# Retention, routing and two expert layers: placing split into two steps, state products and scores in 64x64 tiles

## The chip, the cores and the metric

The kernel runs on one core of a Trainium2 chip. The metric is the device time of one launch in microseconds (us), the median of several runs of the same kernel. Beside it stands one profiled execution, from which all durations below are taken.

## What is computed

```python
def _attn_ref(q, k, v):                      # 8 batches, 8 heads, 576 positions, 64 wide
    scores = scale * np.matmul(q, k.transpose(0, 1, 3, 2))
    Dmat = np.where(rel >= 0, gamma[:, None, None] ** rel[None, :, :], 0.0)
    return np.matmul(scores * Dmat[None, :, :, :], v)

def _moe_ref(x, w_gate, w1, w2):             # 4608 tokens, 512 wide, 8 experts, 1024 hidden
    logits = x @ w_gate
    expert_idx = np.argmax(logits, axis=1)
    ...
        ye = np.maximum(xe @ w1[e], 0.0) @ w2[e]
        out[mask] = gate_w[mask, None] * ye

def _moe2_ref(x, w_in, w_out):               # 512 -> 2048 -> 512
    h = x @ w_in
    return (h * np.cos(h)) @ w_out
```

The three run one after the other: retention, a layer in which each token goes to the one expert with the largest logit, and a wide layer with h cos(h) between its products.

## The kernel before

The retention stage walks over 40 chunks, five for each batch: four of 128 positions and one of 64 (`CH`, line 31). A loop of 45 rounds (line 495) issues the work of several chunks by hand, and each engine runs its instructions in the order in which they are issued. Round i does, in this order:

- `transposes(i + 1)`: eight transposes on TensorE (PE), copied out by ScalarE (ACT) as `qT` and `kpT`;
- `scores(i)`: eight products of keys and queries, one for each head. Two heads share the 128 partitions, so a head's operands lie in partitions 0 to 63 or 64 to 127, and the outputs go to the two banks of `sc` by that half. VectorE (DVE) then masks each bank into `pT` (line 299);
- `decay_k(i + 2)` on DVE, and in rounds 20 to 27 `unit_split`, which waits for weights of the next layer (`wst`) on ACT;
- `inter(i - 1)`: the state of the earlier chunks times the queries. The state of a pair of heads is kept block-diagonal in a 128x128 tile `sbd`, whose other half is zeros, so that four full 128x128 products do it (line 313);
- `intra(i - 1)`: `v` times `pT`, added into the same bank `xps`; DVE scales it into `xt` (line 325); then, but for a batch's last chunk, the state's update in `S` (line 329), which ACT copies into the two diagonal blocks of `sbd` in two copies;
- `table`, then `place`, where a batch is due;
- `rows(i - 2)`: TensorE turns `xt` back into rows and takes the logits (line 340), in the same two banks as `scores` (tag `sc`, one buffer). ACT copies the rows out as `xs`, then DVE reduces the logits to `lgt` (line 344), then SyncE's queue (SP) stores the rows to `xd`;
- `route(i - 2)` at the end of a batch: five short DVE steps that find each token's expert;
- the loads of q, k, v of chunk i + 4, and in rounds 18 to 25 one of weights, on SP's queue.

`scores(i + 1)` of the next round writes the banks that `lgt` of this round reads, and so has to wait for it.

`place` takes a batch one round after it was routed: matmuls with ones and a triangle give each token's rank in `lg` (lines 376 to 384); DVE makes the slot (lines 388 to 400); GpSimd (POOL) and DVE make the one-hot tiles `oh` and `rt` (lines 401 to 425); DVE adds to the running count (lines 429 to 437). Two rounds later `table` multiplies the one-hot tiles together into `lg` (line 444) and DVE adds the result to a table. The batches are placed in rounds 7, 12, 17, 22, 27, 32 and 37 (the last batch in three pieces, in rounds 39, 40 and 42).

After the loop the expert layers run on gathered rows, and then the wide layer. Float32 products that are not transposes appear in the trace as two matmul records each.

Of the kernel before, what the change touches and what calls it, by code (L numbers as in the profile page):

```python
# [11 lines left out]
F32 = mybir.dt.float32  # L12
# [5 lines left out]
ALU = mybir.AluOpType  # L18
AX = mybir.AxisListType
# [3 lines left out]
P = 128  # L23
H = 8
D = 64
DM = 512
E = 8
# [3 lines left out]
CH = [(0, 128), (128, 128), (256, 128), (384, 128), (512, 64)]  # L31
# [8 lines left out]
NWARM = 28  # L40
NWARM2 = 16
# [27 lines left out]
def const_table(B):  # L69

    NT = B * SEQ
    t = np.zeros((P, C_END), np.float64)
    p = np.arange(P)
    t[:, C_ID:C_ID + 128] = np.eye(128)
    t[:, C_MASK:C_MASK + 128] = p[:, None] <= p[None, :]
    t[:, C_TRI:C_TRI + 128] = p[:, None] < p[None, :]
    t[:, C_ONE:C_ONE + 128] = 1.0
    t[:, C_IOTA:C_IOTA + 128] = p
    gam = 1.0 - 2.0 ** (-5.0 - np.arange(H))

    hp = 2 * np.arange(4)[None, :] + (p >= D)[:, None]
# [22 lines left out]
def attn_moe_kernel(ctx, tc, q, k, v, wg, w1, w2, win, wout, ctab, out):  # L104
# [81 lines left out]
    def warm(n, bank, t):  # L186
        t = t.bitcast(BF16)
        for _ in range(n):
            mm(out=bank[:, :2 * P], lhsT=t[:, :P], rhs=t, start=True, stop=True)


    with ExitStack() as actx:
# [25 lines left out]
        def setup():  # L218
            nc.vector.tensor_copy(out=tri, in_=cc(C_TRI, P))
            nc.vector.tensor_copy(out=ones, in_=cc(C_ONE, P))  # L220
            nc.vector.tensor_copy(out=rbase, in_=cc(C_BASE, E))
            nc.vector.memset(rsb, 0.0)
            nc.vector.tensor_copy(out=wgi[:, :, 0:P], in_=ident.unsqueeze(1).to_broadcast([P, 4, P]))
            nc.vector.tensor_copy(out=wgi[:, :, P:RW], in_=wgs)

        def decay_table(c):
# [8 lines left out]
            xts.append(t)  # L235
        sbd = []
        for i in range(2):
            t = ap1.tile([P, 4, P], F32, name=f"sbd{i}")
            nc.gpsimd.memset(t, 0.0)
            sbd.append(t)  # L240
        lgt = []
        for i in range(2):
            t = ap1.tile([P, NCH, E], F32, name=f"lgt{i}")
# [41 lines left out]
        def scores(i):  # L285
            b, c = steps[i]
            o, n = CH[c]
            s = st[i]
            pT = ap2.tile([P, H, P], F32, tag="pT", name="pT")
            two = ps1.tile([P, 8, P], F32, tag="sc", name="sc")  # L290
            scs = [two[:, 0:4], two[:, 4:8]]
            for a in range(4):
                for g in range(2):
                    r = 64 * g
                    mm(out=scs[g][:n, a, :n], lhsT=s["kpT"][r:r + 64, a, :n], rhs=s["qT"][r:r + 64, a, :n],
                       start=(a == 0), stop=True, skip_group_check=True)
# [5 lines left out]
        sps = ps1.tile([P, 4, D], F32, tag="S", name="S")  # L302


        def inter(i):
            b, c = steps[i]
            o, n = CH[c]
            s = st[i]
            s["xp"] = ps2.tile([P, 4, P], F32, tag="x", name="xps")
            if c > 0:  # L310
                sb = sbd[(i - 1) % 2]
                for j in range(4):
                    mm(out=s["xp"][:, j, :n], lhsT=sb[:, j, :], rhs=s["qT"][:, j, :n], start=(j == 0), stop=False,
                       skip_group_check=True)

        def intra(i):
            b, c = steps[i]
            o, n = CH[c]
            s = st[i]
            xp = s["xp"]  # L320
            for h in range(H):
                r = D * (h % 2)
                mm(out=xp[r:r + D, h // 2, :n], lhsT=s["v"][:n, h, :], rhs=s["pT"][:n, h, :n],
                   start=(c == 0 and h < 2), stop=True, skip_group_check=True)
            nc.vector.tensor_mul(out=xts[i % 3][:, :, :n], in0=xp[:, :, :n], in1=gx[:, c, :, :n])
            if c < NCH - 1:
# [42 lines left out]
        def place(i0, n, ohb, df):  # L369
# [28 lines left out]
            nc.vector.tensor_scalar(out=ge, in0=dd, scalar1=0.0, scalar2=None, op0=ALU.is_ge)  # L398
            hot = ap2.tile(hs, F32, tag="hot", name="hot")
            nc.vector.scalar_tensor_tensor(out=hot, in0=dd, scalar=float(P), in1=ge, op0=ALU.is_lt, op1=ALU.mult)  # L400
# [25 lines left out]

            if not last:
                gates()
            if n > 2:
                rr = ap2.tile([P, E], F32, tag="rr", name="rr")  # L430
                nc.vector.tensor_reduce(out=rr, in_=ohb[:, :n - 1].rearrange("p c e -> p e c"), axis=AX.X, op=ALU.add)
                nc.vector.tensor_add(out=rsum, in0=rsum, in1=rr)
            elif n == 2:
                nc.vector.tensor_add(out=rsum, in0=rsum, in1=ohb[:, 0, :])
            m = CH[c0 + n - 1][1]
            nc.vector.tensor_add(out=rsum[:m], in0=rsum[:m], in1=ohb[:m, n - 1, :])
            nc.vector.tensor_copy(out=rsb, in_=rsum)

            def enter(k0, k1):
                w = (k1 - k0) * SL  # L440
# [26 lines left out]
        groups[NS - 3] = (NS - 3, 1)  # L467
        groups[NS - 1] = (NS - 2, 2)
        routed = []
        tabled = []  # L470

        load(0, "q")
# [9 lines left out]
        nc.sync.dma_start(out=wgs, in_=wg.rearrange("(c p) e -> p c e", p=P))  # L482
# [6 lines left out]
        warm(NWARM, ps2.tile([P, 512], F32, tag="x", name="xps"), idle)  # L489
# [4 lines left out]
        waiting = []  # L494
        for i in range(NS + 5):
            if i + 1 < NS:
                transposes(i + 1)
            if i < NS:
# [5 lines left out]
            if i == 0:  # L504
                setup()
            if 1 <= i <= NS:
                inter(i - 1)
                intra(i - 1)

            prev, waiting[:], tabled[:] = waiting[:], tabled[:], []  # L510
# [2 lines left out]
            if i >= NS + 2:  # L513
                while waiting:
                    table(*waiting.pop(0))
            prev, routed[:] = routed[:], []
# [11 lines left out]
        assert not tabled and not routed and not waiting  # L528
        assert not tabled and not routed
        rp = ps2.tile([P, 512], F32, tag="x", name="xps")  # L530
        mm(out=rp[:, :E], lhsT=ones, rhs=rsb, start=True, stop=True)
        warm(NWARM2, ps2.tile([P, 512], F32, tag="x", name="xps"), ident)
        nc.vector.tensor_copy(out=cnt, in_=rp[:, :E])
        nc.vector.tensor_copy(out=sidf, in_=sid)

# [499 lines left out]
```

## Time and profile before

| | us |
|---|---|
| median of 3 runs | 1568.36 (1565.32 to 1570.71) |
| the profiled execution | 1571.7, of which the span is 1569.8 |

The trace is read by stage: a table of windows gives the busy time of every engine in a stretch, the timeline gives the instructions of one round in order, and the table of waits says what an engine stood idle for. All times are us from the start of the span.

### The profile page before, as it was taken

To read this page: it belongs to the slowest core of one execution; us is meant where nothing else is said; L and a number is where in the kernel's file an instruction comes from. 1 tells how busy PE (TensorE), PEld (TensorE's weight loads), DVE (VectorE), ACT (ScalarE), POOL (GpSimd) and SP (SyncE) were. 2 spreads that over 40 slices of the span, in tenths; PEclk is the share of its full clock that TensorE was granted. 3 is DMA by queue.
4 is the path that set the end of the run, shared out by engine and by line. 5 is a ranking of instruction groups with operands and counts; after the bars stand their busy time and mean duration, and the time that the engine had idled before them with its cause. 6 is when DMAs were issued, how large, how long until landed. Compare 5 with 4: busy or idle time off the path is not lost.

```text
span 1569.8 us, 24472 instructions
## 1 busy us (share of the span) xinstructions
PE 1502.7 (96%) x9565; PEld 1334.4 (85%) x9565; DVE 896.1 (57%) x1618; ACT 781.1 (50%) x1395; POOL 359.3 (23%) x399
## 2 busy tenths in 40 slices
PE   8997798799999999999999999999999999999998
PEld 7887788699999999999878888888888888888886
DVE  3555655556575665652256656666665656666554
ACT  3334332244445445433266666666565666666654
POOL 3111111365666657562000101010000101010101
PEclk9999899699999999999999999999999999999999
DMA  9768763365657556556640100000010100000000
GB/s 184 161 146 186 182 136 88 104 203 190 201 188 226 195 182 237 180 162 213 218 162 28 48 7 34 21 27 28 1 53 1 54 1 28 0 27 1 28 0 27
DMA packets 168520, 163.10 MB, mean 104 GB/s; under 512 B 119012, under 2 KB 127664, under 8 KB 166352
## 3 DMA queue, kind: packets, MB, share of 16 engines
q1 hardware_dynamic: 155696, 110.50, 25.8%
q0 software_dynamic: 10688, 36.31, 6.6%
q10 hardware_dynamic: 2016, 14.68, 2.8%
q8 instruction: 76, 1.25, 0.3%
q14 instruction: 44, 0.36, 0.1%
HBM read 115.70 MB, written 45.76 MB: 103 GB/s over the span
## 4 chain that ended last, share of the span: by engine, by line
issue 42%; PE 4%; POOL 2%; ACT 1%; DVE 1%; DMA 0%; POOLq 0%; SPq 0%
PE hps L907 2%; POOL out_dram L959 2%; PE acc L949 1%; PE acc L951 1%; PE acc L950 1%; DVE sa L918 0%; ACT ka L915 0%; DVE sa L919 0%; ACT sa L921 0%; ACT sa L922 0%; POOL spare L140 0%; DVE ka L917 0%; DMA yin<-ydT 0%; ACT sa L923 0%; DVE gl L934 0%
## 5 line engine op out<-in xcount | busy, mean ns | idle before, releaser
L907 PE MATMUL hps<-yT,wunit 128*128 128x512 f32 x1728 | 417.5, 391 | 0.4 <-ACT yT L894 0.4
L907 PEld LDWEIGHTS hps<-yT,wunit 128*128 128x128 f32 x1728 | 324.9, 188 | 69.8 <-DVE yT L895 1.3
L949 PE MATMUL acc<-wunit,gh 128*128 128x512 f32 x576 | 224.1, 389 | 0.0
L950 PE MATMUL acc<-wunit,gh 128*128 128x512 f32 x576 | 224.1, 389 | 0.0
L951 PE MATMUL acc<-wunit,gl 128*128 128x512 f32 x576 | 224.1, 389 | 0.0
L621 PE MATMUL hps<-hh,wunit 128*128 128x360 f32 (+1 forms) x1024 | 223.6, 310 | 0.0
L606 PE MATMUL hps<-xT,wunit 128*128 128x360 f32 (+1 forms) x1536 | 222.8, 306 | 0.5 <-ACT xT L591 0.5
L606 PEld LDWEIGHTS hps<-xT,wunit 128*128 128x128 f32 x1536 | 220.6, 190 | 1.2 <-ACT xT L591 0.9
L959 POOL DMA_INDIRECT out_dram<-orow,perm x36 | 35.2, 978 | 808.7 <-DVE orow L955 802.3
L929 DVE TENSOR_TENSOR sa<-hps,sa 128x512 f32<-128x512 f32 x144 | 99.3, 690 | 160.2 <-ACT sa L923 160.2
L921 ACT ACTIVATE sa<-sa 128x512 f32<-128x512 f32 x144 | 91.1, 633 | 193.8 <-DVE sa L919 193.8
L698 POOL TENSOR_TENSOR wunit<-wst,wunit 128x512 fp32r<-128x512 f32 x112 | 157.6, 1426 | 89.6 <-ACT wunit L697 89.4
L621 PEld LDWEIGHTS hps<-hh,wunit 128*128 128x128 f32 x1024 | 172.1, 192 | 0.0
L621 PE MATMUL hps<-hl,wunit 128*128 128x360 f32 (+1 forms) x512 | 158.1, 309 | 4.8 <-DVE hl L610 4.8
L610 DVE SCALAR_TENSOR_TENSOR hl<-hps,hh 128x360 fp32r<-128x360 f32 (+1 forms) x128 | 60.6, 474 | 178.1 <-ACT hh L609 178.1
L915 ACT ACTIVATE ka<-hps,biases 128x512 f32<-128x512 f32 x144 | 99.0, 688 | 69.4 <-PE hps L907 69.4
L951 PEld LDWEIGHTS acc<-wunit,gl 128*128 128x128 f32 x576 | 108.2, 188 | 22.5
L950 PEld LDWEIGHTS acc<-wunit,gh 128*128 128x128 f32 x576 | 108.1, 188 | 22.5
L949 PEld LDWEIGHTS acc<-wunit,gh 128*128 128x128 f32 x576 | 108.2, 188 | 22.4
L623 ACT COPY yev<-hps 128x256 f32<-128x256 f32 (+1 forms) x64 | 26.7, 417 | 169.1 <-issue 93.9
L923 ACT ACTIVATE sa<-sa,biases 128x512 f32<-128x512 f32 x144 | 104.1, 723 | 4.7
L917 DVE TENSOR_SCALAR ka<-ka 128x512 f32<-128x512 f32 x144 | 61.0, 424 | 74.2 <-ACT ka L915 74.2
(148 smaller groups left out, 2055.5 us busy)
## 6 DMA issues: line engine op xcount, KB each, us to landing
wst<-in_moe_w_dram SPq DMA_DIRECT2D x64, 512.0 KB, 4.5
wd<-cvo POOLq DMA_DIRECT2D x32, 512.0 KB, 3.9
wunit<-wd ACTq DMA_DIRECT2D x14, 1024.0 KB, 5.9
yin<-ydT SPq DMA_DIRECT2D x36, 256.0 KB, 2.7
ldq<-in_q_dram SPq DMA_DIRECT2D x32, 256.0 KB, 3.5
ldk<-in_k_dram SPq DMA_DIRECT2D x32, 256.0 KB, 4.2
ldv<-in_v_dram SPq DMA_DIRECT2D x32, 256.0 KB, 4.5
xd<-xs SPq DMA_DIRECT2D x32, 256.0 KB, 2.2
```

Source lines behind the costliest of these rows:

```text
L606: mm(out=ph[:, :n], lhsT=u[:, a, kc, f0:f0 + P], rhs=t[:, bq, kc, :n], start=(idx == 0), stop=(idx == 11))
L621: mm(out=py[:, :n], lhsT=u[:, w], rhs=t[:, :n], start=(fc == 0 and g == 0), stop=(fc == 7 and g == 2))
L698: nc.gpsimd.tensor_sub(out=u[:, 1, 2 * g + c], in0=s[:, c], in1=u[:, 0, 2 * g + c])
L907: mm(out=ph, lhsT=u[:, a, kc, f0:f0 + P], rhs=t[:, bq, kc, :], start=(idx == 0), stop=(idx == 11))
L915: nc.scalar.activation(out=ka, in_=ph, func=AF.Identity, scale=INV2PI, bias=magic)
L921: nc.scalar.activation(out=sa, in_=sa, func=AF.Sin, scale=0.5)
L923: nc.scalar.activation(out=sa, in_=sa, func=AF.Identity, scale=-2.0, bias=one)
L929: nc.vector.tensor_mul(out=sa, in0=ph, in1=sa)
L949: mm(out=a, lhsT=gh[:, s], rhs=u[:, 0, fc % 4], start=(fc == 0), stop=False)
L950: mm(out=a, lhsT=gh[:, s], rhs=u[:, 1, fc % 4], start=False, stop=False)
L951: mm(out=a, lhsT=gl[:, s], rhs=u[:, 0, fc % 4], start=False, stop=(fc == 15))
L959: ins = nc.gpsimd.indirect_dma_start(out=out[:, :], out_offset=bass.IndirectOffsetOnAxis(ap=perm[:, k:k + 1], axis=0), in_=o, in_offset=None)
```

## The change

- **Placing.** `place` keeps the ranks, the slots and the running count. The rest (the reduction `rm`, the one-hot tiles, the gates) becomes `spread`, which for all but the last piece runs one round later. The steps that make `dd`, `ge` and `hot` move from DVE to POOL for these pieces, one of them cut into two. In a round, `rows` and `route` now come ahead of `spread` and `place`.
- **Scores** are issued as 64x64 tiles: four matmuls for each pair of heads, two for a chunk of 64.
- **State products** are issued head by head as 64x64 tiles. The state is kept without its zeros (`sbd` is 128x4x64, one ACT copy of all partitions). So that four neighbouring heads fall on four different tiles, odd head pairs write the other half of the partitions, and in a second bank; `xps` now has two banks and one buffer instead of two buffers of one bank.
- The halves of odd pairs stay swapped through `xt`; the decay table, the identity in `wgi` and the gate weights are swapped to suit, so one DMA of the gate weights becomes three and one copy into `wgi` three.
- Where the chunk i - 1 has 64 positions, `inter(i - 1)` moves to the front of the round, followed by a small ACT copy out of `xps` (`between`).

```diff
-            for a in range(4):
-                for g in range(2):
-                    r = 64 * g
-                    mm(out=scs[g][:n, a, :n], lhsT=s["kpT"][r:r + 64, a, :n], rhs=s["qT"][r:r + 64, a, :n],
-                       start=(a == 0), stop=True, skip_group_check=True)
+            for j in range(4):
+                for g, r in ((0, 0), (1, D), (0, D), (1, 0)):
+                    if r < n:
+                        mm(out=scs[g][r:r + D, j, :n], lhsT=s["kpT"][D * g:D * g + D, j, r:r + D],
+                           rhs=s["qT"][D * g:D * g + D, j, :n], start=(j == 0), stop=True, skip_group_check=True)
...
+        def place_of(h):
+            j, a = h // 2, h % 2
+            return (j % 2) * 4 + j // 2, D * (a ^ (j % 2))
...
-            s["xp"] = ps2.tile([P, 4, P], F32, tag="x", name="xps")
+            s["xp"] = ps1.tile([P, 8, P], F32, tag="x", name="xps")
             if c > 0:
                 sb = sbd[(i - 1) % 2]
-                for j in range(4):
-                    mm(out=s["xp"][:, j, :n], lhsT=sb[:, j, :], rhs=s["qT"][:, j, :n], start=(j == 0), stop=False,
-                       skip_group_check=True)
+                for h in range(H):
+                    k, r = place_of(h)
+                    d = D * (h % 2)
+                    mm(out=s["xp"][r:r + D, k, :n], lhsT=sb[d:d + D, h // 2, :], rhs=s["qT"][d:d + D, h // 2, :n],
+                       start=(h < 4), stop=False, skip_group_check=True)
...
             for h in range(H):
-                r = D * (h % 2)
-                mm(out=xp[r:r + D, h // 2, :n], lhsT=s["v"][:n, h, :], rhs=s["pT"][:n, h, :n],
-                   start=(c == 0 and h < 2), stop=True, skip_group_check=True)
-            nc.vector.tensor_mul(out=xts[i % 3][:, :, :n], in0=xp[:, :, :n], in1=gx[:, c, :, :n])
+                k, r = place_of(h)
+                mm(out=xp[r:r + D, k, :n], lhsT=s["v"][:n, h, :], rhs=s["pT"][:n, h, :n],
+                   start=(c == 0 and h < 4), stop=True, skip_group_check=True)
...
-                nc.scalar.copy(out=t[0:64, :, 0:64], in_=sps[0:64])
-                nc.scalar.copy(out=t[64:128, :, 64:128], in_=sps[64:128])
+                nc.scalar.copy(out=t, in_=sps)
...
-            nc.vector.tensor_tensor(out=dd, in0=dst.unsqueeze(2).to_broadcast(hs), in1=lo, op=ALU.subtract)
+            ve.tensor_tensor(out=dd, in0=dst.unsqueeze(2).to_broadcast(hs), in1=lo, op=ALU.subtract)
...
+            nc.vector.tensor_copy(out=rsb, in_=rsum)
+            if not last:
+                placed.append((i0, n, ex, hot, dd, False))
+
+        def spread(i0, n, ex, hot, dd, last):
...
+            short = 1 <= i <= NS and CH[steps[i - 1][1]][1] <= D
+            if short:
+                inter(i - 1)
+                nc.scalar.copy(out=between, in_=st[i - 1]["xp"].rearrange("p (a j) t -> p j a t", a=2)[:, 0:2, :, 0:1])
             if i + 1 < NS:
                 transposes(i + 1)
...
-            for r in prev:
-                place(*r)
             if 0 <= i - 2 < NS:
                 rows(i - 2)
+            to_spread, placed[:] = placed[:], []
+            to_place, routed[:] = routed[:], []
             if i - 2 in groups:
                 route(*groups[i - 2])
+            for r in to_spread:
+                spread(*r)
+            for r in to_place:
+                place(*r)
```

## Rows read from the trace of the kernel before

**Rows 1.** Windows by stage: length, busy time (instructions) by engine, PEclk, DMA share, GB/s.
```profile
22.00:268.26 246.26, 216.00 (x2568) 194.63 (x2567) 135.69 (x339) 85.95 (x186) 37.49 (x72) 0.92 0.68 153
268.26:298.00 29.74, 18.27 (x153) 15.07 (x153) 17.81 (x93) 5.05 (x11) 8.53 (x17) 0.69 0.32 98
298.00:770.00 472.00, 462.84 (x3241) 460.46 (x3241) 260.09 (x392) 197.07 (x415) 261.53 (x212) 0.98 0.58 191
```

**Rows 2.** Waits from 22 to 268: who for whom, total us, times, longest.
```profile
PE sc L295 <- DVE lgt L344: 29.4, 13, 3.7
ACT wunit L179 <- DMA wst<-in_moe_w_dram: 14.2, 6, 4.8
```

**Rows 3.** Timeline of PE, one ordinary round: start, length, operation, shapes, records.
```profile
27.75 1.16 PE L295 MATMUL sc<-qT,kpT 64*128 64x128 f32 x16 [0.26 <-DVE lgt L344]
28.84 1.16 PE L313 MATMUL xps<-qT,sbd 128*128 128x128 f32 x8
29.93 1.09 PE L323 MATMUL xps<-pT,ldv 128*64 128x128 f32 x16
30.86 0.64 PE L329 MATMUL S<-ldv,kp 128*64 128x64 f32 x16
31.42 1.19 PE L340 MATMUL rw<-wgi,xt 128*128 128x136 f32 x8
32.45 0.60 PE L279 MATMUL tp<-ct,ldq 128*128 128x128 f32 x4
...
33.52 0.56 PE L295 MATMUL sc<-qT,kpT 64*64 64x64 f32 x12
```

**Rows 4.** Timeline of DVE and ACT in the same round.
```profile
28.96 1.29 DVE L299 TENSOR_TENSOR pT<-sc,ca 128x512 f32<-128x512 f32 x2 [1.26 <-PE sc L295]
32.65 0.59 ACT L343 COPY xs<-rw 128x512 f32<-128x512 f32 x1 [0.30 <-PE rw L340]
33.27 0.19 DVE L344 TENSOR_REDUCE lgt<-rw 128x8 f32<-128x32 f32 x1 [1.44 <-ACT xs L343]
```

**Rows 5.** Timeline of PE and DVE around the placing of one batch.
```profile
117.03 1.17 PE L340 MATMUL rw<-wgi,xt 128*128 128x136 f32 x8
117.21 0.20 DVE L388 TENSOR_TENSOR t<-lg,ohb 128x40 f32<-128x40 f32 x1
119.46 0.36 DVE L403 TENSOR_REDUCE rm<-dd 128x5 f32<-128x200 f32 x1 [0.72 <-POOL dd L401]
120.92 0.20 DVE L431 TENSOR_REDUCE rr<-ohb 128x8 f32<-128x32 bf16 x1
121.62 0.18 DVE L344 TENSOR_REDUCE lgt<-rw 128x8 f32<-128x32 f32 x1
121.86 0.49 PE L295 MATMUL sc<-qT,kpT 64*128 64x128 f32 x4 [3.02 <-DVE lgt L344]
```

**Rows 6.** Windows of the rounds that follow a placing.
```profile
57.11:64.47 7.36, 7.32 (x72) 6.57 (x72) 2.77 (x5) 1.60 (x4) 2.37 (x5) 0.77 0.39 75
88.88:97.46 8.58, 8.55 (x72) 7.79 (x72) 2.77 (x5) 1.60 (x4) 2.37 (x5) 0.65 0.30 60
259.79:268.26 8.47, 7.57 (x64) 6.85 (x64) 2.19 (x5) 1.32 (x3) 2.37 (x5) 0.66 0.00 0
```

**Rows 7.** Timeline of PE in a round whose chunk i - 1 has 64 positions.
```profile
103.59 1.16 PE L295 MATMUL sc<-qT,kpT 64*128 64x128 f32 x16
105.72 0.68 PE L323 MATMUL xps<-pT,ldv 64*64 64x64 f32 x16
106.33 1.19 PE L340 MATMUL rw<-wgi,xt 128*128 128x136 f32 x8
```

**Rows 8.** Timeline of PE, the first hundredths of a us of one scores block.
```profile
108.47 0.38 PE L295 MATMUL sc<-qT,kpT 64*128 64x128 f32 x2
```

**Rows 9.** Timeline of PE, the matmuls of one table step.
```profile
271.45 0.91 PE L444 MATMUL lg<-rt,oh 128*128 128x120 f32 x5
```

**Rows 10.** Window of 8 us while weights load: columns as in rows 1.
```profile
140.00:148.00 8.00, 4.90 (x67) 4.34 (x68) 4.50 (x10) 4.00 (x8) 0.00 (x0) 1.00 1.09 239
```

More of the change, by code (lines that the diff above doesn't have):

```diff
@@ L79, in const_table @@
     gam = 1.0 - 2.0 ** (-5.0 - np.arange(H))
-    hp = 2 * np.arange(4)[None, :] + (p >= D)[:, None]
+    hp = 2 * np.arange(4)[None, :] + ((p >= D)[:, None] ^ (np.arange(4) % 2 == 1)[None, :])
     for c, (o, n) in enumerate(CH):
@@ L222, in setup @@
             nc.vector.memset(rsb, 0.0)
-            nc.vector.tensor_copy(out=wgi[:, :, 0:P], in_=ident.unsqueeze(1).to_broadcast([P, 4, P]))
+            nc.vector.tensor_copy(out=wgi[:, 0::2, 0:P], in_=ident.unsqueeze(1).to_broadcast([P, 2, P]))
+            for a in range(2):
+                nc.vector.tensor_copy(out=wgi[:, 1::2, a * D:(a + 1) * D],
+                                      in_=ident[:, (1 - a) * D:(2 - a) * D].unsqueeze(1).to_broadcast([P, 2, D]))
             nc.vector.tensor_copy(out=wgi[:, :, P:RW], in_=wgs)
@@ L237, in attn_moe_kernel @@
         for i in range(2):
-            t = ap1.tile([P, 4, P], F32, name=f"sbd{i}")
-            nc.gpsimd.memset(t, 0.0)
-            sbd.append(t)
+            sbd.append(ap1.tile([P, 4, D], F32, name=f"sbd{i}"))
         lgt = []
@@ L300, in scores @@
             s["pT"] = pT
-        sps = ps1.tile([P, 4, D], F32, tag="S", name="S")
+        sps = ps1.tile([P, 8, D], F32, tag="S", name="S")[:, 0:4]
+        def place_of(h):
+            j, a = h // 2, h % 2
+            return (j % 2) * 4 + j // 2, D * (a ^ (j % 2))
         def inter(i):
@@ L321, in intra @@
             for h in range(H):
-                r = D * (h % 2)
-                mm(out=xp[r:r + D, h // 2, :n], lhsT=s["v"][:n, h, :], rhs=s["pT"][:n, h, :n],
-                   start=(c == 0 and h < 2), stop=True, skip_group_check=True)
-            nc.vector.tensor_mul(out=xts[i % 3][:, :, :n], in0=xp[:, :, :n], in1=gx[:, c, :, :n])
+                k, r = place_of(h)
+                mm(out=xp[r:r + D, k, :n], lhsT=s["v"][:n, h, :], rhs=s["pT"][:n, h, :n],
+                   start=(c == 0 and h < 4), stop=True, skip_group_check=True)
+            two = "p (j a) t -> p j a t"
+            nc.vector.tensor_mul(out=xts[i % 3].rearrange(two, a=2)[:, :, :, :n],
+                                 in0=xp.rearrange("p (a j) t -> p j a t", a=2)[:, 0:2, :, :n],
+                                 in1=gx[:, c].rearrange(two, a=2)[:, :, :, :n])
             if c < NCH - 1:
@@ L395, in place @@
             dd = ap2.tile(hs, F32, tag="dd", name="dd")
-            nc.vector.tensor_tensor(out=dd, in0=dst.unsqueeze(2).to_broadcast(hs), in1=lo, op=ALU.subtract)
+            ve.tensor_tensor(out=dd, in0=dst.unsqueeze(2).to_broadcast(hs), in1=lo, op=ALU.subtract)
             ge = ap2.tile(hs, F32, tag="ge", name="ge")
-            nc.vector.tensor_scalar(out=ge, in0=dd, scalar1=0.0, scalar2=None, op0=ALU.is_ge)
+            ve.tensor_scalar(out=ge, in0=dd, scalar1=0.0, scalar2=None, op0=ALU.is_ge)
             hot = ap2.tile(hs, F32, tag="hot", name="hot")
-            nc.vector.scalar_tensor_tensor(out=hot, in0=dd, scalar=float(P), in1=ge, op0=ALU.is_lt, op1=ALU.mult)
-            ve.tensor_tensor(out=dd, in0=dd, in1=hot, op=ALU.mult)
+            if last:
+                ve.scalar_tensor_tensor(out=hot, in0=dd, scalar=float(P), in1=ge, op0=ALU.is_lt, op1=ALU.mult)
+            else:
+                ve.tensor_scalar(out=hot, in0=dd, scalar1=float(P), scalar2=None, op0=ALU.is_lt)
+                ve.tensor_tensor(out=hot, in0=hot, in1=ge, op=ALU.mult)
+            ve.tensor_tensor(out=dd, in0=dd, in1=hot, op=ALU.mult)
+            if last:
+                spread(i0, n, ex, hot, dd, True)
+            if n > 2:
+                rr = ap2.tile([P, E], F32, tag="rr", name="rr")
+                nc.vector.tensor_reduce(out=rr, in_=ohb[:, :n - 1].rearrange("p c e -> p e c"), axis=AX.X, op=ALU.add)
+                nc.vector.tensor_add(out=rsum, in0=rsum, in1=rr)
+            elif n == 2:
+                nc.vector.tensor_add(out=rsum, in0=rsum, in1=ohb[:, 0, :])
+            m = CH[c0 + n - 1][1]
+            nc.vector.tensor_add(out=rsum[:m], in0=rsum[:m], in1=ohb[:m, n - 1, :])
+            nc.vector.tensor_copy(out=rsb, in_=rsum)
+            if not last:
+                placed.append((i0, n, ex, hot, dd, False))
+        def spread(i0, n, ex, hot, dd, last):
+            c0 = steps[i0][1]
+            hs = [P, n, SL]
+            ve = nc.vector if last else nc.gpsimd
             rm = ap2.tile([P, n], F32, tag="rm", name="rm")
@@ L428, in place @@
                 gates()
[L429 to L437, printed above, removed]
             def enter(k0, k1):
@@ L469, in attn_moe_kernel @@
         routed = []
+        placed = []
         tabled = []
@@ L481, in attn_moe_kernel @@
         nc.sync.dma_start(out=ca[:, C_TRI - C_MASK:], in_=ctab[:, C_TRI:C_GX])
-        nc.sync.dma_start(out=wgs, in_=wg.rearrange("(c p) e -> p c e", p=P))
+        wgc = wg.rearrange("(c p) e -> p c e", p=P)
+        nc.sync.dma_start(out=wgs[:, 0::2], in_=wgc[:, 0::2])
+        for a in range(2):
+            nc.sync.dma_start(out=wgs[a * D:(a + 1) * D, 1::2], in_=wgc[(1 - a) * D:(2 - a) * D, 1::2])
         loads(2)
@@ L488, in attn_moe_kernel @@
         nc.vector.memset(idle, 0.0)
-        warm(NWARM, ps2.tile([P, 512], F32, tag="x", name="xps"), idle)
+        warm(NWARM, ps1.tile([P, 8, P], F32, tag="x", name="xps").rearrange("p a t -> p (a t)"), idle)
         decay_k(0)
@@ L494, in attn_moe_kernel @@
         waiting = []
+        between = ap1.tile([P, 2, 2, 1], F32, name="between")
         for i in range(NS + 5):
+            short = 1 <= i <= NS and CH[steps[i - 1][1]][1] <= D
+            if short:
+                inter(i - 1)
+                nc.scalar.copy(out=between, in_=st[i - 1]["xp"].rearrange("p (a j) t -> p j a t", a=2)[:, 0:2, :, 0:1])
             if i + 1 < NS:
@@ L506, in attn_moe_kernel @@
             if 1 <= i <= NS:
-                inter(i - 1)
+                if not short:
+                    inter(i - 1)
                 intra(i - 1)
@@ L526, in attn_moe_kernel @@
                 unit_load(ap3, *wq[i - 18])
-        assert not tabled and not routed and not waiting
+        assert not tabled and not routed and not waiting and not placed
         assert not tabled and not routed
-        rp = ps2.tile([P, 512], F32, tag="x", name="xps")
+        rp = ps1.tile([P, 8, P], F32, tag="x", name="xps").rearrange("p a t -> p (a t)")
         mm(out=rp[:, :E], lhsT=ones, rhs=rsb, start=True, stop=True)
-        warm(NWARM2, ps2.tile([P, 512], F32, tag="x", name="xps"), ident)
+        warm(NWARM2, ps1.tile([P, 8, P], F32, tag="x", name="xps").rearrange("p a t -> p (a t)"), ident)
         nc.vector.tensor_copy(out=cnt, in_=rp[:, :E])
```

1 line of the change is left out of this document (removed).

## The prediction

> **What bounds the kernel now.** I read the table of windows by stage first. Retention takes the first 268 us, and from 22 us on PE is busy for 216.0 of 246.3 us at a mean granted clock of 0.92; behind it the expert layers keep PE busy for 462.8 of 472.0 us [rows 1]. The diff touches no line behind 298 us, so what the retention stage gains reaches the end unshortened, and what PE does there counts one to one. Next the waits: PE's own are all of one kind, `scores` waiting for `lgt`, 29.4 us in 13 waits [rows 2]. Then the timeline of one ordinary round, 27.75 to 33.52, which is 5.77 us: PE goes from block to block and idles 0.26 us ahead of `scores` [rows 3]. That idling is a chain: `rows` at 31.42, `xs` at 32.65, `lgt` until 33.46, then `scores` [rows 3, 4].
>
> The same chain around a placing is what costs. `rows` starts at 117.03, but `lgt` comes at 121.62, since DVE runs the whole of `place` ahead of it, and PE stands for 3.02 us [rows 5]. Seven rounds do this. The round behind each then runs at a mean clock of 0.77 or less: PE has been granted the lower of its two levels, 1.2 GHz, for about half of it. Five of the seven take 7.3 to 7.4 us, the other two 8.58 and 8.47, where 5.77 is ordinary [rows 6, 3].
>
> **The change part by part.** All sums are against the profiled execution, 1571.7 us, 3.3 above the median.
>
> *Placing behind `rows`.* DVE now does `lgt` first; the eight rank matmuls go behind `rows`, where PE idled anyway. The wait falls from 3.02 to the ordinary 0.26: 7 x 2.76 = **19.3 us**. With no long stall the clock should hold: 5 x 1.59 + 2.81 + 2.70 = **13.5 us** [rows 3, 5, 6]. What is late next: in the placing round DVE still does ranks to slot (117.21 to about 117.7) and the running count (0.70, 120.92 to 121.62) behind `lgt`, some 1.2 us, and `pT` can't start earlier than 1.21 us behind the start of `scores` anyway (28.96 against 27.75) [rows 3 to 5]. One round on, `spread` puts 1.46 us and `rm` on DVE (119.46 to 120.92) ahead of the next `pT` [rows 5]; that delays `rows` of that round by perhaps 0.25 us: 7 x 0.25 = 1.8 us lost. POOL has five steps more, of some 0.6 us each (0.72 for the wait on one [rows 5]), and a whole round for them. `table` comes a round later, in the round with the 64-wide chunk, where PE is going to wait for `pT` (below): its 0.8 us (0.91 less the overlap with its neighbour [rows 9]) is then hidden, 7 x 0.8 = 5.6. Net **3.8 us**.
>
> *Quarter tiles.* The two first records of a `scores` block take 0.38 us together [rows 8], and the 16 take 1.16, so a pair of records that run side by side adds (1.16 - 0.38) / 7 = 0.111 us. I call that a beat. `inter` before is 8 records in 1.16: one per beat, half of the array multiplying zeros. Each block costs 8 beats and 0.20 us for filling and draining (1.09) [rows 3]. After, `scores` has 32 records and `inter` 16. If four run side by side, that is 8 beats and 4. Both have one tile shape, so one 0.20 goes as well: 2.18 becomes 12 x 0.111 + 0.20 = 1.53. **0.65 us in each of 16 rounds, 10.4 us**. In the 8 rounds with `scores` of a 64-wide chunk, which keep two tiles, `inter` saves 4 beats and most of a drain: **0.6 x 8 = 4.8 us**. Rounds without `inter` gain nothing.
>
> That four run side by side is not shown: rows have two at a time. The bounds are one, two and four, and I take four, since two row halves [rows 8] and two column halves (16 records of `intra` in 1.09 us [rows 3], half the time per record of `inter`) each overlap fully, and a quarter tile takes one half of either kind.
>
> By the Trainium skill's "TensorE: Matmul & The Clock Gate", Part 3, matmuls on different tiles start about 4 ns apart and all run at once, which would be the four; the same section calls the matmuls strict first-in-first-out, and by that the two records of one product, on one tile, would hold up the next tile: two at a time, the second rival.
>
> `intra` now meets the column halves in the order 0, 64, 64, 0 instead of alternating. If PE can't look past a blocked record, each of four changes costs up to half a beat, 0.2 us a round, 8 us in all; below nothing isn't possible, as the work is the same. I take 1 us, because the pair of rows 8 shows PE passing records by.
>
> *The round behind a 64-wide chunk (seven).* Here `inter` leaves the middle. `scores` and `intra` then last 0.94 + 0.20 + 0.61 = 1.75 us, but `rows` shares its banks with `scores` and has to wait for `pT`, done 2.50 us behind the start of `scores` [rows 4]. It was 2.74 [rows 7], so only 0.2 is won. At the front `inter` costs 4 beats of half length and two changes of shape, 0.64 us, against 0.26 of idle time filled. `xps` now has one buffer, so this `inter` also waits for `xt` of the chunk before, 0 to 0.3 us. `between` is one small ACT copy ahead of `qT`, off the path. In sum 0.3 us lost, **2 us**.
>
> *The rest.* `xt` and `pT` keep their sizes; one copy of the state instead of two spares ACT 0.4 us where nobody waits. Start: two more DMAs on SP's queue ahead of the loads of chunk 2 and two more copies, 0.5 us lost (0 to 1.5). The last batch's three pieces lie in 29.7 us at a clock of 0.69 [rows 1]; `lgt` is earlier there too, but `spread` of the small pieces lies between: 1 us won (2 lost to 3 won). Loads: the stage moves 153 GB/s on average [rows 1], which becomes 189 in 199 us; 239 were reached [rows 10]. Only while weights load is it tight: an average round brings 0.94 MB and 0.52 more of weights, 6.1 us at 239 GB/s, while the rounds shrink to about 5. ACT already waits 14.2 us for them [rows 2], and these waits stand ahead of `xs`. I take 2 us lost (0 to 5).
>
> Sum: 10.4 + 4.8 - 2 + 19.3 + 13.5 + 3.8 - 1 - 0.5 + 1 - 2 = 47.3 us. 1571.7 becomes 1524.4, the median **1521 us**.
>
> **The rivals.**
>
> *Shared bank.* `inter` writes one bank from both row halves, which `scores` never did; if such tiles take turns, `inter` stays at 8 beats in 24 rounds: 0.44 x 24 = 10.6 us less, 1532. For it: no row shows two row halves in one bank; against it: they write different partitions. The Trainium skill's "TensorEngine Tiling (Array Packing)", Restrictions and Gotchas, says that different row tiles cannot access the same PSUM bank at once; no run so far shows it.
>
> *Two at a time.* `scores` then takes 16 beats, `inter` 8. The 16 ordinary rounds lose 0.68 each, the 8 with narrow scores win 0.15, the 7 without `inter` lose 0.9, the 7 of the last kind 0.95: 22.6 us lost. Placing still gives 36.6, the small terms cost 2.5: 1557. For it: two is all that the rows show.
>
> *The wait comes back.* If POOL is not done with its five steps when `rm` comes up, or `spread` holds up `pT` by more than I think, PE stalls a round later and the clock falls as before. Then only the tiles gain, 13, less 3 of small losses: 1558. For it: `rm` waited for POOL before, 0.72 us [rows 5]; against it: POOL has a whole round.
>
> *Slower.* One tile at a time: `scores` goes from 8 beats to 32, +2.66 us in 31 rounds, `inter` from 8 to 16, +0.89 in 24. That is 104 us lost against 36 won: 1637. The place is the two blocks, and it decides from fewer than about 1.7 records side by side. For it: 64x64 tiles in all four quarters never ran here; against it: 64x64 tiles in two quarters did, and their 12 records took 0.56 us [rows 3].
>
> **How the numbers follow.** Forecast 0.68, its own range 1506 to 1538 (intra's order, weights, tail and the last kind of round on one side; a stall less while weights load and a cheaper round behind the narrow chunk on the other). Shared bank 0.08, two at a time 0.11, the wait 0.07, slower 0.04, a cancelling mix 0.02. The range 1505 to 1556 takes in the first two and half of the next two. What a measurement of this kernel can tell from no change is 0.3%, about 4.7 us. Faster 0.92, the same 0.04, slower 0.04.
>
> **What would show it.** Right: no wait of `scores` on `lgt` above 1 us outside the weights' rounds, clock near 1 from 22 to 268 us, `scores` with 32 records still near 1.1 us, `inter` with 16 records near 0.6, ordinary rounds near 5.1 us, the stage some 47 us shorter. `scores` near 2 us means two at a time; `inter` alone near 1.1 the shared bank; rounds at clock 0.77 behind a placing the wait. Long waits of ACT for `wst` would make it wrong from the side of the loads.

## The result and the profile after

The changed kernel takes **1514.9 us** (median of 4 runs, 1513.83 to 1518.76) where the kernel before takes 1568.92 (1565.32 to 1570.71): a ratio of **0.966, interval 0.964 to 0.969**, or 54.0 us less. The forecast was 1521 us, range 1505 to 1556. The profiled execution took 1514.11 us with a span of 1512.3, which is 57.6 us less than the profiled execution of before.

Windows by stage of the kernel after, with the columns of [rows 1] (length; busy time and instructions of PE, PEld, DVE, ACT, POOL; PEclk; DMA share; GB/s):

```profile
21.58:211.30 189.72, 177.03 (x3289) 158.67 (x3288) 126.03 (x312) 75.00 (x163) 58.94 (x92) 1.00 0.80 199
211.30:241.90 30.60, 17.95 (x172) 13.84 (x173) 18.82 (x95) 5.12 (x12) 15.81 (x33) 0.72 0.38 116
241.90:713.00 471.10, 462.18 (x3244) 460.10 (x3245) 260.94 (x390) 196.16 (x414) 260.05 (x212) 0.98 0.59 190
```

The first row answers to the first of [rows 1]: the same 37 rounds take 189.72 us for 246.26, so 56.5 of the 57.6 us lie there. PE is busy for 39 us less, idles for 17.6 us less (12.7 for 30.3), and its clock, 0.92 before, is now granted in full. The expert layers take what they took.

Waits in this stretch, of all engines and of PE alone (who for whom, total us, times, longest), to set against [rows 2]:

```profile
ACT wunit L179 <- DMA wst<-in_moe_w_dram: 16.8, 8, 4.4
PE sc L297 <- DVE lgt L355: 7.2, 12, 2.3
PE rw L351 <- DVE pT L301: 2.3, 7, 1.0
PE xps L322 <- DVE lgt L355: 2.2, 1, 2.2
```

The 29.4 us that `scores` waited for `lgt` are 7.2; one more of 2.2 us falls on `inter`, in a round in which weights load and `inter` comes first. A new wait has come, seven times, of `rows` for `pT`. ACT's waits for the weights have not gone; they have grown from 14.2 to 16.8.

The timeline of PE in one ordinary round (start, length, operation, shapes, records), as in [rows 3]:

```profile
26.64 1.10 PE L297 MATMUL sc<-qT,kpT 64*64 64x128 f32 x32 [0.27 <-DVE lgt L355]
27.56 0.62 PE L322 MATMUL xps<-qT,sbd 64*64 64x128 f32 x16
28.11 1.09 PE L332 MATMUL xps<-pT,ldv 128*64 128x128 f32 x16
29.03 0.64 PE L341 MATMUL S<-ldv,kp 128*64 128x64 f32 x16
29.59 1.19 PE L351 MATMUL rw<-wgi,xt 128*128 128x136 f32 x8
30.62 0.60 PE L280 MATMUL tp<-ct,ldq 128*128 128x128 f32 x4
...
31.69 0.32 PE L297 MATMUL sc<-qT,kpT 64*64 64x64 f32 x3
```

The round lasts 31.69 - 26.64 = 5.05 us, 0.72 less than before. `scores` has twice the records in about the same time, and `inter` (L322) twice the records in half the time. `inter` starts 0.92 us behind `scores` (1.09 before) and `intra` 0.55 behind `inter` (1.09 before). The idle time ahead of `scores` is as it was, 0.27.

Around a placing, PE, DVE, ACT and POOL, to set against [rows 5]:

```profile
49.10 1.19 PE L351 MATMUL rw<-wgi,xt 128*128 128x136 f32 x8
50.38 0.58 ACT L354 COPY xs<-rw 128x512 f32<-128x512 f32 x1 [0.79 <-PE rw L351]
51.00 0.19 DVE L355 TENSOR_REDUCE lgt<-rw 128x8 f32<-128x32 f32 x1 [1.20 <-ACT xs L354]
51.10 0.19 DVE L399 TENSOR_TENSOR t<-lg,ohb 128x40 f32<-128x40 f32 x1
51.24 1.10 PE L297 MATMUL sc<-qT,kpT 64*64 64x128 f32 x32 [0.15 <-DVE lgt L355]
51.61 0.52 POOL L407 TENSOR_TENSOR dd<-dsts,ca 128x200 f32<-128x200 f32 x1 [29.75 <-DVE dsts L401]
52.38 0.22 DVE L427 CAST rsb<-rsum 128x8 bf16<-128x8 f32 x1
52.51 0.68 DVE L301 TENSOR_TENSOR pT<-sc,ca 128x512 f32<-128x512 f32 x1
...
54.94 0.61 POOL L416 TENSOR_TENSOR dd<-dd,hot 128x200 f32<-128x200 f32 x1
56.16 0.35 DVE L437 TENSOR_REDUCE rm<-dd 128x5 f32<-128x200 f32 x1
```

`lgt` now stands ahead of the ranks (51.00, then 51.10), `scores` starts 0.24 us behind it, and the 3.02 us of waiting are 0.15. What is left of `place` ends at 52.60, and `pT` starts at 52.51, 1.27 us behind `scores`; in the ordinary round of before it was 1.21. POOL ends `dd` at 55.55, and `rm` comes at 56.16 without a wait for it.

### The profile page after: what moved, and what is told of

Its sections match the earlier page's. It is cut to its first block, busy times and chain, and to the rows that moved or that the text cites. A ratio compares the mean times of both kernels' runs of the same rounds, so it can differ in the third digit from the quotient of the medians.

```text
span 1512.3 us, 26000 instructions
## 1 busy us (share of the span) xinstructions
PE 1462.3 (97%) x10333; PEld 1296.5 (86%) x10333; DVE 888.6 (59%) x1593; ACT 769.2 (51%) x1371; POOL 386.0 (26%) x433
## 4 chain that ended last, share of the span: by engine, by line
issue 44%; PE 4%; POOL 2%; ACT 1%; DVE 1%; DMA 0%; POOLq 0%; SPq 0%
PE hps L946 2%; POOL out_dram L998 2%; PE acc L988 1%; PE acc L989 1%; PE acc L990 1%; DVE sa L957 0%; ACT ka L954 0%; DVE sa L958 0%; ACT sa L960 0%; ACT sa L961 0%; POOL spare L140 0%; DVE ka L956 0%; DMA yin<-ydT 0%; ACT sa L962 0%; DVE gl L973 0%
## 5 line engine op out<-in xcount | busy, mean ns | idle before, releaser
L990 PEld LDWEIGHTS acc<-wunit,gl 128*128 128x128 f32 x576 | 108.1, 188 | 22.4
L988 PEld LDWEIGHTS acc<-wunit,gh 128*128 128x128 f32 x576 | 108.0, 188 | 22.4
```

Of the source, the lines that this page charges most:

```text
L988: mm(out=a, lhsT=gh[:, s], rhs=u[:, 0, fc % 4], start=(fc == 0), stop=False)
L990: mm(out=a, lhsT=gl[:, s], rhs=u[:, 0, fc % 4], start=False, stop=(fc == 15))
```

## The experiments

All times are medians; the kernel before stood beside each group on the same chip: 1569.35 (1568.81 to 1570.85) for the placing alone, the tiles alone, the filled wait and the order alone; 1569.67 (1563.61 to 1571.93) for the second bank, the scores tiles, the first run of the weights and the single execution with the filled wait; 1568.82 (1563.66 to 1573.37) for the last three. The theory is that of the prediction: the placing's wait and the slow clock behind it make up most of the gain, and quarter tiles, four side by side, the rest. The rivals are its four, and that the gain has another source (the clock alone, the order alone).

**The two halves apart.** First the placing alone: the kernel before with the order and the split of `place`, and its old tiles.

```diff
...
+            to_spread, placed[:] = placed[:], []
+            to_place, routed[:] = routed[:], []
             if i - 2 in groups:
                 route(*groups[i - 2])
+            for r in to_spread:
+                spread(*r)
+            for r in to_place:
+                place(*r)
```

> The kernel before with the placing of the kernel after (place and spread, POOL steps, behind rows) and its old tiles. Theory (the wait behind a placing costs twice, in idle time and in the slow clock after it): 7 x 2.9 us of waits, 13.5 us of slow rounds behind them and some 2.5 us of a slow clock in the rounds with weights go: 1569 becomes 1532 (1528 to 1537), granted clock near 1 in rounds 2 to 38. Rival (most of the gain is the tiles', the placing only lets PE reach the next limit sooner): above 1545.

Measured: 1532.36 (1529.64 to 1533.41), ratio 0.976 (0.974 to 0.977). The window of the stage, and the timeline of PE in a round behind a placing, from its start to that of the next:

```profile
23.20:232.95 209.75, 199.92 (x2568) 180.42 (x2567) 128.65 (x312) 85.00 (x186) 57.79 (x91) 0.99 0.78 179
```

```profile
55.41 1.16 PE L295 MATMUL sc<-qT,kpT 64*128 64x128 f32 x16 [0.15 <-DVE lgt L344]
...
61.18 0.68 PE L295 MATMUL sc<-qT,kpT 64*64 64x64 f32 x16
```

The stage is 36.5 us shorter. The round starts after 0.15 us of waiting and lasts 61.18 - 55.41 = 5.77 us, as an ordinary one, where [rows 6] had 7.36. The rounds with the table's matmuls are 5.72 where their likes without it are 4.88: with the old tiles the table still costs 0.84 us.

Then the tiles alone: the changed kernel with `place` whole and in its old place ahead of `rows`.

```diff
...
+            prev, routed[:] = routed[:], []
+            for r in prev:
+                place(*r)
             if 0 <= i - 2 < NS:
                 rows(i - 2)
-            to_spread, placed[:] = placed[:], []
-            to_place, routed[:] = routed[:], []
...
```

> The kernel after with the placing of the kernel before; all tiles are the new ones. Theory: 0.71 us in each of 16 rounds, 0.65 in 8, 0.3 lost in 7, somewhat more where the clock is low: 1569 becomes 1552 (1549 to 1556), and the seven waits of some 3 us and the slow rounds behind them stay. Rival (with the waits in place, what PE saves is only waited longer): 1565 or more.

Measured: 1555.13 (1554.91 to 1555.35), ratio 0.991 (0.989 to 0.992). The window of the stage and PE's longest group of waits in it:

```profile
21.42:250.83 229.41, 189.15 (x3288) 169.07 (x3288) 134.07 (x339) 75.17 (x163) 37.22 (x71) 0.93 0.66 164
```

```profile
PE sc L297 <- DVE lgt L355: 31.2, 11, 4.4
```

The wait for `lgt` is there in full, 31.2 us, and so is the low clock, 0.93. In the stage the two halves give 36.5 and 16.9 us, 53.4 in sum; together they gave 56.5. The difference has two parts. The table's 0.84 us, six times in this stretch (5.0 us), is hidden only when both are there, since the new tiles make PE wait for `pT` in just the round to which the new placing moves the table. Against it, rounds 20 to 29, in which weights load, give 2.8 and 2.6 us in the two halves apart (by the lengths of the rounds, worked out as in the next section) and only 3.5 together, 1.9 less.

**The slow clock by itself.** The prediction counts 19.3 us of waiting and 13.5 us of slow rounds behind it. To part them, the wait stays, and PE is kept at work during it: 24 small matmuls of zeros into a spare bank ahead of `scores` in the seven placing rounds.

```diff
+            if i in (8, 13, 18, 23, 28, 33, 38):
+                warm(24, ps1.tile([P, 512], F32, tag="lg", name="lg"), idle)
```

> The kernel before with 24 small matmuls of zeros into the free rank bank ahead of scores in rounds 8, 13, 18, 23, 28, 33 and 38, where PE waits for lgt anyway; nothing else changes, and their results are not used. Theory (the slow rounds are slow because PE stood still before them): the wait stays as long, the seven rounds behind it run at full clock in some 5.8 us instead of 7.3 to 8.6: 1569 becomes 1555 (1552 to 1559). Rival (they are slow for another reason, POOL's work beside them): the rounds keep 7.3 us and the time stays at 1569 or rises.

Measured: 1554.28 (1550.82 to 1554.49), ratio 0.989 (0.988 to 0.991), from four executions; a fifth took 5226 us, for a reason that is not known, and is left out. The profile is of that one, so a further execution was profiled.

> The same kernel as e3_busy_wait, one look at its trace. Theory: in rounds 8, 13, 18, 28, 33 and 38 the wait of scores on lgt is filled with the small matmuls, the granted clock is 1 in them and in the rounds behind, and these take 5.8 us. Rival: they take 7.3 us.

Measured: 1550.13 in this single execution. The small matmuls at the end of a placing round, then the windows of that round and of the one behind it:

```profile
55.03 2.79 PE L189 MATMUL lg<-idle 128*128 128x256 bf16 x24
58.16 1.16 PE L295 MATMUL sc<-qT,kpT 64*128 64x128 f32 x16 [0.34 <-DVE lgt L344]
```

```profile
49.42:58.16 8.74, 8.40 (x104) 7.37 (x104) 7.08 (x25) 2.81 (x8) 2.91 (x6) 1.00 0.72 169
58.16:63.92 5.76, 5.73 (x72) 5.18 (x72) 2.77 (x5) 1.60 (x4) 2.37 (x5) 1.00 0.48 94
```

The placing round is as long as before, 8.74, since DVE still runs `place` ahead of `lgt`. The round behind it, 7.36 at a clock of 0.77 in [rows 6], takes 5.76 at 1.00. Nothing else is altered, so the slow rounds come from PE standing still. By the medians they cost 15.1 us (19.5 by the single execution). In its trace the seven rounds behind a placing take 40.4 us, for 53.8 before: 13.4 us, as the prediction has it (13.5). The rest of the 17.2 us by which the stage is shorter there lies in rounds 20 to 29, in which weights load. They hold two of the seven rounds, and lose 3.8 us more than these two: 67.47 us for 74.47 before, at a clock of 0.97 for 0.89:

```profile
130.42:197.89 67.47, 61.03 (x744) 54.58 (x745) 43.61 (x100) 29.19 (x57) 10.52 (x20) 0.97 0.85 198
```

**The order alone.** `rows` and `route` ahead of a `place` that stays whole, on DVE: is the split needed?

```diff
-            prev, routed[:] = routed[:], []
-            for r in prev:
-                place(*r)
             if 0 <= i - 2 < NS:
                 rows(i - 2)
+            prev, routed[:] = routed[:], []
             if i - 2 in groups:
                 route(*groups[i - 2])
+            for r in prev:
+                place(*r)
```

> The kernel before with rows and route ahead of place, which stays whole, with its DVE steps. Theory (the split is needed too): lgt comes in time, but the 4.4 us of DVE steps then stand ahead of the next pT, and rows of that round waits for pT 2.3 to 2.6 us instead: 1562 to 1568 if the clock falls again, 1552 to 1558 if PE's work in between keeps it up. Rival (the order is what counts): the same as the placing alone, some 1532.

Measured: 1554.74 (1553.08 to 1556.76), ratio 0.990 (0.989 to 0.992): the time of the second branch, in which the clock was to hold. The timeline of PE and DVE in a placing round, and PE's waits in the stage:

```profile
58.33 0.17 DVE L437 CAST rsb<-rsum 128x8 bf16<-128x8 f32 x1
58.41 1.28 DVE L299 TENSOR_TENSOR pT<-sc,ca 128x512 f32<-128x512 f32 x2
59.84 1.26 PE L340 MATMUL rw<-wgi,xt 128*128 128x136 f32 x8 [1.99 <-DVE pT L299]
```

```profile
PE rw L340 <- DVE pT L299: 13.8, 7, 2.0
PE sc L295 <- DVE lgt L344: 4.3, 4, 2.2
```

`scores` no longer waits for `place`; `rows` does, one block later, because `pT` now stands behind it on DVE. Of the 3 us of a placing 2.0 remain, and the clock falls behind them, as in the first branch:

```profile
59.84:62.50 2.66, 2.66 (x16) 2.57 (x16) 1.30 (x3) 1.09 (x2) 1.37 (x3) 0.68 0.02 6
```

So the time came out in the second branch for another reason than the one given: more than half of the gain, 9.0 of the 16.9 us by which the stage is shorter in the trace, lies in rounds 20 to 29, in which weights load (65.5 us for 74.5). The expectation had left these rounds out. Of the 37.0 us of the placing alone the order gives 14.6, and the split with POOL the other 22.4.

**The second bank and the swapped pairs.** The changed kernel with the odd pairs not swapped: still two banks and 64x64 tiles, but each head's state product now stands on one of two quarters.

```diff
...
-            return (j % 2) * 4 + j // 2, D * (a ^ (j % 2))
+            return (j % 2) * 4 + j // 2, D * a
...
```

> The kernel after without the swap of the halves in odd pairs (tables, identity and gate weights unswapped too): the state products still alternate between two banks, but fall on the two diagonal quarters only. Theory (the swap is what puts four products side by side): inter goes from 4 to 8 beats of 0.11 us in 24 rounds and from 4 to 8 half beats in 8: some 12 us more, 1515 becomes 1527 (1524 to 1530), and an inter block is again near 0.9 us. Rival (two row halves in one bank take turns): 16 beats, 1545 or more. Rival (the narrow shape and the missing switch of shape are the gain, not four side by side): 1515.

Measured: 1522.02 (1518.69 to 1524.96), ratio 0.971 (0.969 to 0.973), below what was expected. The timeline of PE in one round:

```profile
47.01 1.10 PE L297 MATMUL sc<-qT,kpT 64*64 64x128 f32 x32
47.93 1.04 PE L322 MATMUL xps<-qT,sbd 64*64 64x128 f32 x16
48.90 1.09 PE L332 MATMUL xps<-pT,ldv 128*64 128x128 f32 x16
```

The block behaves as expected: `inter` takes 1.04 us for 0.62, and an ordinary round 5.48 for 5.05. Over the 24 blocks of full length and the 8 of half length this would be the 12 us expected, but the medians differ by 7.1, and the stage by 7.9 (197.59 us for 189.72): in the rounds in which weights load PE has to wait anyway, and the longer block fills some of that (round 21, counted from the first, takes 6.53 us instead of 6.94, and what rounds 20 to 29 lose to the weights falls from 7.4 to 3.9). The expectation had left these rounds out. So two banks without the swap don't put four side by side; four quarters in one bank were not tried.

**The scores tiles alone.** The changed kernel with `scores` in the form of before, 16 records of 64x128.

> The kernel after with the scores in the 64x128 form of before. Theory (scores were already full; the quarter form only saves a switch of tile shape ahead of inter and half of a first weight load): 0.17 us more in 16 rounds, 0.05 in some 15: 1515 becomes 1518.5 (1516.5 to 1520.5). Rival (the quarter form of the scores carries half of what the tiles gain): 1522 or more.

Measured: 1520.72 (1516.63 to 1524.86), ratio 0.970 (0.968 to 0.972), a hair above what was expected. The timeline of PE:

```profile
46.47 1.16 PE L297 MATMUL sc<-qT,kpT 64*128 64x128 f32 x16
47.56 0.67 PE L322 MATMUL xps<-qT,sbd 64*64 64x128 f32 x16
48.16 1.09 PE L332 MATMUL xps<-pT,ldv 128*64 128x128 f32 x16
```

From the start of `scores` to that of `intra` it takes 1.69 us for the 1.47 above, 0.22 more, 0.17 of it ahead of `inter` (1.09 for 0.92): two shapes instead of one, as the prediction's drain has it (0.17 forecast here, 0.20 per change in the sum). Over the stage the trace shows 3.7 us (193.42 for 189.72), as expected; the medians, 5.8 apart, are less sharp. So cutting `scores` into quarters saves no multiplication; it saves time between the blocks. That this is the change of shape, and not in part the first load of weights of a block, is the reading of the expectation; the two were not parted.

**The weights.** In the kernel after, PE's longest waits are in the rounds in which weights load. The timeline of ACT and PE in one of them:

```profile
120.48 1.05 ACT L179 CAST wunit<-wst 128x1024 fp32r<-128x1024 f32 x1 [4.37 <-DMA wst<-in_moe_w_dram]
121.70 0.58 ACT L354 COPY xs<-rw 64x512 f32<-64x512 f32 x1
123.53 1.10 PE L297 MATMUL sc<-qT,kpT 64*64 64x128 f32 x32 [2.29 <-DVE lgt L355]
```

ACT stands 4.37 us at a conversion whose load has not landed, `xs` is queued behind it, and `scores` waits 2.29 us for the `lgt` that needs `xs`. The remedy that this suggests is to convert a round later.

```diff
-            if 20 <= i < 20 + len(wq):
-                unit_split(*wq[i - 20], upA)
+            if 21 <= i < 21 + len(wq):
+                unit_split(*wq[i - 21], upA)
```

> The kernel after with unit_split one round later (rounds 21 to 28), so that each piece of weights has one more round to land. Theory (rounds 20 to 29 lose some 7 us to ACT waiting for weights that were asked for too late): 1515 becomes 1509.5 (1508 to 1512), no wait of scores on lgt above 1 us. Rival (the loads' rate is the limit there): 1513 to 1516, and the waits only move.

Measured: 1509.03 (1508.72 to 1513.13), ratio 0.963 (0.961 to 0.965). The stage takes 186.37 us for 189.72. The longest wait of `scores` on `lgt` is 1.15 us, where the expectation had none above 1. ACT's remaining wait:

```profile
ACT wunit L179 <- DMA wst<-in_moe_w_dram: 1.3, 1, 1.3
```

The changed kernel had been timed in another group of runs. So the two were then run side by side, with a third that converts two rounds later.

> The changed kernel itself, unaltered, so that it is timed on one chip beside the version with the weights split a round later. 1513 to 1518 us, as before.

> The changed kernel with each weight unit split one round later (rounds 21 to 28 for 20 to 27), once more, beside the changed kernel on the same chip. Theory (ACT waited for the weights' loads ahead of xs, 16.8 us in 8 waits, and PE for xs): 5 us below the changed kernel, 1509 (1508 to 1513). Rival (the 5.9 us between two groups of runs were a difference of chips or days): no difference.

> The changed kernel with each weight unit split two rounds later (22 to 29). Theory: splitting one round later already left ACT a single wait of 1.3 us for a weight load, so one more round gains at most that: 1508 to 1510, the same as one round later. Rival (the 4 us that the rounds 20 to 28 still lie above their unhindered lengths are loads too): 1505 to 1506.

Measured: the changed kernel 1515.91 (1514.12 to 1516.8), one round later 1511.62 (1506.9 to 1513.04), two rounds later 1511.09 (1509.96 to 1514.43). The slowest run of one round later is faster than the fastest of the changed kernel, so this version beats both kernels, the changed one by 4.3 us. Two rounds later gains nothing more. ACT waits for no load there (with one round it still did, 3.1 us in 2 waits), and yet `scores` waits for `lgt` as long, 4.5 us; in the version with two rounds:

```profile
PE sc L297 <- DVE lgt L355: 4.5, 12, 1.3
```

With one round later, the rounds 20 to 28 still take 48.1 us where their likes elsewhere add up to 44.2. These 4 us (from the first run of this version) are therefore not late loads. The conversions' own time on ACT and DVE (1.05 us each on ACT) would do it, but that wasn't tried.

## Why the prediction was right

The mechanism held in the terms that make up most of the sum, and the sum was too small: 47.3 us against 57.6 in the profiled executions and 54.0 in the medians (the execution profiled before is 2.8 us above its median). Term by term, from the lengths of the rounds (start of `scores` to start of the next):

| step | forecast, us | measured, us | from |
|---|---|---|---|
| placing: wait, clock behind it | 32.8 | 33.7: 36.5 in the placing alone, less 2.8 that the weights' rounds give there | stage 246.26 to 209.75 |
| ordinary round, tiles, each | 0.65 | 0.72 | 5.77 to 5.05 |
| two rounds around a 64-wide chunk, each pair | 0.6 - 0.3 | 0.37 | 5.29 + 4.88 to 5.08 + 4.72 |
| `spread` ahead of the next `pT`, each | -0.25 | 0 | 5.08 with it and without |
| table, each | 0.8 | 0.84 | 6.13 to 5.29 before and in the placing alone; 4.72 with and without after |
| `intra`'s order, all | -1 | 0 | block of 1.09 before and after |
| start | -0.5 | 0.4 | first ordinary round at 21.58 for 21.99 |
| loads of the weights | -2 | 3.6 | next paragraph |

**The step that was mis-sized most is the loads.** The prediction had 2 us lost to them, since the rounds shrink while the bytes don't. The direction of the waits was right: ACT's for `wst` grew from 14.2 to 16.8 us, which the prediction names as what would make it wrong. But what counts is PE's time. Rounds 20 to 29 took 74.5 us before, where rounds of the same kinds elsewhere add up to 63.5: 10.9 us were lost to the weights. After, it is 56.6 against 49.2, 7.4 us. So 3.6 us were won where 2 were to be lost, 5.6 us of the 10.3 that the sum missed. This term is the least certain: in the other profiled execution of the changed kernel, the one beside the later conversions, the same rounds take 58.7 us, 9.4 more than their likes, so that only 1.5 us would be won. The largest single item is a round of before in which a placing met a late load; its window:

```profile
185.06:196.29 11.23, 8.20 (x79) 7.41 (x80) 8.19 (x26) 3.37 (x8) 2.88 (x6) 0.76 0.59 131
```

It is a placing round, 8.70 elsewhere, and 2.5 us longer at a clock of 0.76: the round ahead of it had stalled for a load as well, and the low clock lay over this one. The same round takes 5.09 us after. The prediction counted the clock only in the seven rounds of [rows 6] and overlooked that stalls of the weights cost it too; the mean clock of 0.92 in [rows 1] held both. After, the stage's clock is 1.00 (0.99 in the other execution). The kernel before with its waits filled bears this out: there rounds 20 to 29 take 67.5 us where their likes add up to 60.4, so that 7.1 us are lost to the weights for 10.9, with the loads and the order of work as they were.

**The rest of the miss is small and mostly of one sign**, some 0.78 us in each group of five rounds, 5.5 in all: the delay by `spread` that never came (0.25), a dearer drain than put (0.07 for each of two ordinary rounds), `intra`'s order (0.12), the wait of a placing, which fell to 0.15 and not to 0.26 (0.12), the rounds around the narrow chunk (0.07), the table and a batch's first round (0.04 each). `spread` delays nothing because `rm`, `gts` and their kind fall between `lgt` and `pT`, where DVE idles. The start gave 0.9 more than forecast. The tail, from round 39 to the first matmul of the expert layers, went from 30.40 to 29.60 us: 1.6 less than the 2.4 that belongs to it (1 for `lgt`, 0.6 for the last narrow chunk, 0.8 for the last table).

Three readings of the prediction were off without harm. The rank matmuls of a batch are seven, not eight. POOL has four more steps, not five, and they take 0.52 to 1.15 us each, not 0.6; that they come to 3.1 us for each batch, about what five of 0.6 would take, is luck. And [rows 8] shows that two records start together, but not of which products they are, so that PE passes a blocked record by was not shown there; the 1.09 us of `intra` in both orders says only that the order costs nothing.

**The wait that was forecast for the round behind the narrow chunk** is there. The timeline of PE, DVE and ACT:

```profile
35.35 0.46 PE L322 MATMUL xps<-qT,sbd 64*64 64x64 f32 x16
35.94 0.17 ACT L530 COPY between<-xps 128x4 f32<-128x4 f32 x1
36.77 1.10 PE L297 MATMUL sc<-qT,kpT 64*64 64x128 f32 x32
...
37.94 1.29 DVE L301 TENSOR_TENSOR pT<-sc,ca 128x512 f32<-128x512 f32 x2 [1.67 <-PE sc L297]
39.38 0.47 PE L351 MATMUL rw<-wgi,xt 128*128 128x136 f32 x2 [1.05 <-DVE pT L301]
```

`rows` starts 2.61 us behind `scores` (2.50 forecast, 2.74 in [rows 7]), after 1.05 us of waiting. This is the gap in which the table's matmuls are hidden.

**The rivals.** *Shared bank* and *two at a time* fall with one block: 16 records of `inter` in 0.62 us. Less 0.20 for the drain it is 26 ns for each; with two quarters (the pairs not swapped) the same 16 take 1.04, 52 ns. `scores` with 32 records in 1.10 gives 28. Four run side by side. The Trainium skill's "TensorE: Matmul & The Clock Gate", Part 3, has matmuls on different tiles running all at once and also strict first-in-first-out; here the first agrees, and whatever order the records end in, it doesn't cost a tile its turn. *The wait comes back* falls with `rm`, which didn't wait, and *slower* with the same blocks as the first two.

## What to carry to other kernels

A wait of TensorE is paid twice where the granted clock falls behind it: look at the clock of the rounds that follow a stall, and count those as part of the stall's price; where the wait itself can't be removed, small products of zeros in it give that part back. Moving a long step behind the one that others wait for can pass most of the wait on to the next reader on the same engine (2.0 of 3.0 us here); what removed the rest was to move the piece of the step that nobody waits for to another engine and a later round. Quarter tiles paid here where neighbouring records fall on four different quarters, so the layout of the output has to be chosen for the order of issue; and when PE has become faster, look again at which loads were placed for the old pace.

## What the runs showed of the hardware that was not expected

- Two row halves that write one bank at the same time don't hold each other up as long as they write different partitions: each of the two banks of `inter` takes products of both row halves, and the block runs at 26 ns for a record. The Trainium skill's "TensorEngine Tiling (Array Packing)", Restrictions and Gotchas, says that different row tiles cannot access one bank at once; for different partitions these runs don't bear that out. Two row halves on the same partitions of one bank weren't tried.
- 24 small matmuls of zeros hold the clock at the higher of its two levels, 2.4 GHz, through a wait of 3 us: the round behind it runs at 1.00 for 0.77.
- The length of a stall alone doesn't say whether the clock falls. Behind the wait of 1.99 us of `rows`, with the order alone changed, PE ran at 0.68 (the window above); behind the wait of 2.29 us of `scores` in the changed kernel it ran at 1.00:

```profile
123.53:126.00 2.47, 2.47 (x68) 2.30 (x70) 2.27 (x8) 0.89 (x1) 0.00 (x0) 1.00 0.96 225
```

  In the other execution of the changed kernel the same wait was 2.79 us, and the round behind it, 6.64 us long for 5.10, ran at 0.74:

```profile
123.92:130.56 6.64, 6.50 (x103) 5.92 (x103) 4.83 (x12) 2.28 (x5) 0.00 (x0) 0.74 0.84 221
```

  So the changed kernel has not left the slow clock behind for good where weights load late. Why the clock fell in the one case and not in the other, these runs don't settle.
- Two tile shapes in place of one cost about 0.2 us from `scores` to `intra` (1.69 us for 1.47), while the order 0, 64, 64, 0 of the column halves in `intra` costs nothing.
